# A fused attention and two-expert-layer kernel: V spread over partitions by way of DRAM, and the split of one half of the last rows at another step

## The chip, the cores and the metric

The kernel runs on one core of one Trainium2 chip. The metric is the device time of one execution in microseconds. The engines are named TensorE (PE; PEld is its weight load), VectorE (DVE), ScalarE (ACT), GpSimd (POOL) and SyncE (SP); SyncE issues most of the DMAs.

## The reference

Three stages follow one another. All sizes are fixed: batch 4, 8 heads, 576 positions, head dimension 64, 128 random features, model width 512, 8 experts.

```python
def phi(x):
    proj = np.einsum('bhsd,df->bhsf', x, w_phi)
    proj = proj - np.max(np.abs(proj), axis=-1, keepdims=True)
    return np.concatenate([np.exp(proj), np.exp(-proj)], axis=-1)
q_p, k_p = (phi(q), phi(k))
kv = np.einsum('bhsf,bhsd->bhfd', k_p, v)
z = np.sum(k_p, axis=2)
num = np.einsum('bhsf,bhfd->bhsd', q_p, kv)
den = np.einsum('bhsf,bhf->bhs', q_p, z)[..., None] + 1e-06
x = num / den                       # then heads side by side: [4, 576, 512]
...
h = x.transpose(0, 2, 1) @ U @ V    # U [576, 32], V [32, 576]: mixes positions
u = x + h.transpose(0, 2, 1)
x = u + np.maximum(u @ w_ch1, 0.0) @ w_ch2      # inner width 2048
...
# per position: an expert e of 8 (argmax, or the previous one's), its softmax share p
out[b, s] = p[e] * (np.maximum(x[b, s] @ w1[e], 0.0) @ w2[e])   # inner width 1024
```

U, V, `w_ch1` and `w_ch2` arrive in float64 and are narrowed on the chip.

## The kernel before

**Stages.** `attn_step(S_)` runs the attention as a software pipeline over 16 pairs of heads: projections (`proj`, tile `pj`), exponentials (`exp_k` into `ek`, `tq` into `eq`), `kv_mm`, `num`, then `t_mm` (tile `tps`, product with U) and `ut` (tile `utps`, transposed back to rows of features, plus the product with V). `ut` writes `y`, which holds u transposed: 512 features as 4 x 128 partitions, by 2304 rows (4 x 576 positions). Then `work()` runs the blocks of the two feed-forward layers: `mm1` multiplies by the first layer's weights into PSUM tile `psf`, `mm2` by the second's. Four units of weights are gone through by five blocks of 512, 512, 256, 512 and 512 rows each.

**Precision by halves.** A float32 value x is held as two reduced-precision numbers, `hi` (a cast of x) and `lo` (x minus `hi`), and each product takes three matmuls: weight-hi by hi, weight-hi by lo, weight-lo by hi (lines 537 to 539 and 556 to 558). So before `mm1` can read rows, those rows of `y` need a cast on ScalarE (`hi_a`, `hi_b`, line 510) and a subtraction on GpSimd (`lo_a`, `lo_b`, line 512, four instructions of 128 x 288). `split_rows(b, c)` does that for half c of batch b; half (3,0) are rows 1728 to 2015. `mm1` of the fourth block (rows 1280 to 1791) is the first that reads it. In the same way `mm1`'s results go to `hhi` (line 542, ScalarE) and `hlo` (line 543, VectorE), which `mm2` reads.

**V.** `load_uv` is a generator that `attn_step` and `prepare` advance: U and V are loaded, narrowed (VectorE, and an addition on GpSimd, line 76), and V, which arrives as 4 chunks of 144 columns, each on its own 32 partitions (`vq`), is spread so that each of four groups of 32 partitions holds all 576 columns (`v`). `vs` is its float32r form: the cast (line 273) in all groups, and in the second and fourth group the remainder (line 275). `ut` reads it from the seventh step on.

**The order of the work.** It is written out by hand. Each engine runs its instructions in the order of the program text. During `work()` the function `side(i, step)` places side work behind step 0 to 7 of block i: at steps 2 and 6 it takes the next entry of `splits`, and it advances the preparation of a weight tile (`w_prep`: conversions on VectorE, an addition into `cv_w` on GpSimd, a cast on ScalarE at line 173, a subtraction into `w` on GpSimd). At the end of the attention (1,1) and (2,0) are split at once, and `splits` holds (2,1), (3,0), (3,1). The first block is done by then, so the second block's steps take (2,1) and (3,0) and the third block's step takes (3,1).

**PSUM.** `tq`, `num`, `tps`, `utps` and V's products `vps` share one pool of three buffers (`ps_f`): each new tile waits until the tile three before it has been read. In the feed-forward stages five buffers go round.

Of the kernel before, what the change touches and what calls it, by code (L numbers as in the profile page):

```python
# [7 lines left out]
F32 = mybir.dt.float32  # L8
# [8 lines left out]
B, H, S, D, F = 4, 8, 576, 64, 128  # L17
# [22 lines left out]
def model(ctx, tc, kq, vx, wphi, ident, up, vp, wff, wg, wmoe, rconst, outT):  # L40
    nc = tc.nc
# [8 lines left out]
    dram = ctx.enter_context(tc.tile_pool(name="dram", bufs=1, space=bass.MemoryType.DRAM))  # L50
    ula_p = ctx.enter_context(tc.tile_pool(name="ula", bufs=1))
    ps_f = ctx.enter_context(tc.tile_pool(name="ps_f", bufs=3, space=PSUM))

    def f32(ap):
        return ap.bitcast(F32)

    id_sb = const.tile([128, 128], F32, name="id_sb")
# [163 lines left out]
    spare = y.rearrange("p k t -> p (k t)").rearrange("p (r s) -> p r s", s=S)  # L221
# [25 lines left out]
    def load_uv():  # L247


        u, v, vq = spare[:, 10, :160], spare[:, 14], spare[:, 11, :144]  # L250
        four = spare[:, 15, :512].rearrange("p (c r j) -> p c r j", c=4, r=4)
        u_load, u_convert = load_small(up, 128, 160)
        v_load, v_convert = load_small(vp, 128, 144)
        next(u_load)
        next(v_load)
        yield
        u_convert(u)
        for c in range(4):
            nc.gpsimd.tensor_copy(out=four[:, c], in_=id_sb[:, 32 * c:32 * c + 32].unsqueeze(1).to_broadcast([128, 4, 32]))
        u3 = u.rearrange("p (c r) -> p c r", c=5)  # L260
        for c in (0, 32):
            nc.gpsimd.tensor_copy(out=ur[:, :, c:c + 32], in_=u3)
        yield
        v_convert(vq)
        yield
        for h in range(2):
            ps = ps_f.tile([128, 2, 144], F32, tag="f", name="vps")
            for c in range(2):
                nc.tensor.matmul(ps[:, c], lhsT=four[:, 2 * h + c].rearrange("p r j -> p (r j)"), rhs=vq,
                                 start=(c == 0), stop=(c == 1), skip_group_check=True)  # L270
            nc.scalar.copy(out=v[:, 288 * h:288 * h + 288].rearrange("p (c s) -> p c s", c=2), in_=ps)
        yield
        nc.scalar.copy(out=vs, in_=v)
        for r in (slice(32, 64), slice(96, 128)):
            nc.gpsimd.tensor_tensor(out=vs[r], in0=v[r], in1=f32(vs[r]), op=ALU.subtract)

    early = [load_uv()]
    next(early[0])
    load_v(1)
# [422 lines left out]
    splits = []  # L702

    def side(i, step):

        u, _, _, c = blocks[i]
        if u.kind == "ffn":
            if splits and step in (2, 6):
                split_rows(*splits.pop(0))
            if u.g < 3:  # L710
                for _ in range(2 if step in (3, 7) else 1):
                    if not preps and room() and at["prep"] < min(8 * u.g + 16, 8 * u.g + 10 + 8 * c // 5 if u.g else 16):
                        preps.append(w_prep())
                    prep_step()
                if late:
                    w_ahead()
            else:
                if step == 0 and c > 1:
                    bg.append(route(c - 2))
                bg_step()  # L720
                if 0 not in pidx:
                    bg_step()
                if 0 in pidx and step in (1, 3, 4, 5, 7):
                    if at["prep"] < 8 * len(ffn_units) + 8 and room():
                        preps.append(w_prep())
                        drain(preps)
                        w_ahead()
        else:
            k = units.index(u)
            if i + 2 == n and step == 0:  # L730

                drain(bg)
                left = late["ul"].tile([1, 1], F32, name="left")
                late["left"] = late["ul"].tile([1, 1], I32, name="lefti")
                nc.vector.tensor_reduce(out=left, in_=late["flags"], axis=AX, op=ALU.add)
                nc.vector.tensor_copy(out=late["left"], in_=left)
            if u.b == 0 and u.g == 0 and c == 0 and step == 0:
                bg.append(route(3))
            bg_step()
            if c == 0 and step == 4 and u.g == 0:  # L740
                scale_row(u.b)
            if k + 1 < len(units) and at["prep"] < min(8 * (k + 2), 8 * k + 8 + 4 * c + (step + 1) // 2) and room():
                v = units[k + 1]
                if v.b not in pidx:
                    drain(bg)
                preps.append(w_prep())
                drain(preps)
                w_ahead()
# [81 lines left out]
    with tc.For_i(0, nl):  # L830
# [42 lines left out]
        ps = late["psr"].tile([128, 4], F32, tag="r1", bufs=2, name="l_mps")  # L873
# [3 lines left out]
        for c in range(2):  # L877
            sl = slice(c * CH, (c + 1) * CH)
            for k, into in ((0, yb[:, :, sl]), (1, ob[:, :, sl])):
                h, l = (f32(t)[:, :, bass.ds(at_[k][c] * CH, CH)] for t in ul[k])  # L880
# [6 lines left out]
        with tc.For_i(0, FT2) as j:  # L887
# [3 lines left out]
            for c in range(2):  # L891
                sl = slice(c * CH, (c + 1) * CH)
                ps = late["psg"].tile([128, CF], F32, tag="f", name="l_ps")[:, :CH]
# [4 lines left out]
                for d in range(4):  # L898
                    ps = ps_f.tile([128, CF], F32, tag="f", name="l_acc")[:, :CH]
# [79 lines left out]
```

## Time and profile before

| | |
|---|---|
| runs, us | 797.07, 797.0, 795.45; median 797.0 |
| profiled execution, us | 795.62, of which the span is 793.8 |
| busy share of the span | PE 98%, PEld 87%, DVE 57%, ACT 34%, POOL 24% |
| granted TensorE clock, mean | 0.996 |
| TensorE's share of the chain that ended last | 88% |

A time in the sections below counts from the start of the span. The chain that ended last is followed back from the last instruction, at each step to whatever released it. The busy shares are means over stages of different kinds: until about 205 us the attention runs, with VectorE and ScalarE close to full in its first part; behind it the feed-forward layers are nearly all TensorE.

### The profile page before, as it was taken

The page shows a single profiled execution, that of the slowest core. Times are in us where ns is not written, and L with a number is a line of the kernel's source. Part 1 is how long each engine was busy: PE and PEld are TensorE (multiplying, and loading weights), DVE is VectorE, ACT ScalarE, POOL GpSimd, SP SyncE. Part 2 cuts the span into 40 slices and gives each one's busy share as a digit, 9 for nine tenths or more (in the row PEclk, how much of TensorE's full clock was granted, in tenths as well). Part 3 has the DMA queues.
Part 4 walks back from the last instruction along what each step waited for, and adds up shares of the span by engine and source line. Part 5 has one row for each costly group of instructions (what it writes and reads, how often), then busy time and mean ns, then how long its engine had stood idle before and what let it go on. Part 6 is the DMA issues. An engine that isn't in the chain of part 4 may idle for free.

```text
span 793.8 us, 17863 instructions
## 1 busy us (share of the span) xinstructions
PE 780.9 (98%) x7492; PEld 694.3 (87%) x7492; DVE 454.9 (57%) x889; ACT 269.0 (34%) x589; POOL 190.9 (24%) x242
## 2 busy tenths in 40 slices
PE   8999999999999999999999999999999999999997
PEld 6899888988888888988889888887889999999997
DVE  7888999742675535544555443246567664434442
ACT  5667777741221111111111111122324433243340
POOL 1122424200474202230222302021204441202202
PEclk9999999999999999999999999999999999999999
DMA  6444434200012101110011100001222342343421
GB/s 198 149 123 142 130 112 143 64 2 2 27 53 78 44 12 53 54 54 23 30 54 54 54 0 1 1 1 39 58 69 70 103 127 90 110 131 110 128 71 62
DMA packets 25778, 56.04 MB, mean 71 GB/s; under 512 B 3616, under 2 KB 8864, under 8 KB 25696
## 3 DMA queue, kind: packets, MB, share of 16 engines
q1 hardware_dynamic: 21984, 51.28, 20.6%
q10 hardware_dynamic: 3456, 3.46, 1.3%
q8 instruction: 59, 0.97, 0.5%
q0 software_dynamic: 256, 0.15, 0.1%
q14 instruction: 23, 0.19, 0.1%
HBM read 50.01 MB, written 4.87 MB: 69 GB/s over the span
## 4 chain that ended last, share of the span: by engine, by line
PE 88%; DVE 7%; ACT 2%; POOL 2%; DMA 1%; issue 1%; DVEq 0%; ACTq 0%
PE psf L539 12%; PE psf L556 12%; PE psf L537 12%; PE psf L538 12%; PE psf L557 12%; PE psf L558 12%; PE kv L332 4%; PE num L366 3%; PE pj L299 3%; PE tq L346 2%; DVE pg L303 2%; DVE mx L302 1%; POOL lo_b L512 1%; PE utps L409 1%; PE tps L392 1%; PE utps L404 1%
## 5 line engine op out<-in xcount | busy, mean ns | idle before, releaser
L556 PE MATMUL psf<-hhi,w 128*128 128x512 f32 (+2 forms) x576 | 194.2, 337 | 0.0
L557 PE MATMUL psf<-hhi,w 128*128 128x512 f32 (+2 forms) x576 | 193.3, 336 | 0.3 <-DVE w L177 0.3
L558 PE MATMUL psf<-hlo,w 128*128 128x512 f32 (+2 forms) x576 | 193.1, 335 | 0.0
L543 DVE SCALAR_TENSOR_TENSOR hlo<-psf,hhi 128x512 fp32r<-128x512 f32 (+2 forms) x144 | 80.1, 556 | 178.4 <-ACT hhi L542 178.3
L542 ACT ACTIVATE hhi<-psf 128x512 fp32r<-128x512 f32 (+2 forms) x144 | 70.7, 492 | 261.8 <-PE psf L539 254.1
L556 PEld LDWEIGHTS psf<-hhi,w 128*128 128x128 f32 x576 | 108.3, 188 | 12.1 <-issue 1.4
L538 PE MATMUL psf<-lo_b,w 128*128 128x288 f32 (+2 forms) x352 | 116.0, 329 | 1.8 <-POOL lo_b L512 1.8
L557 PEld LDWEIGHTS psf<-hhi,w 128*128 128x128 f32 x576 | 108.3, 188 | 10.5 <-DVE w L177 0.5
L558 PEld LDWEIGHTS psf<-hlo,w 128*128 128x128 f32 x576 | 108.3, 188 | 10.3
L539 PE MATMUL psf<-hi_b,w 128*128 128x288 f32 (+2 forms) x352 | 116.4, 331 | 0.0
L537 PE MATMUL psf<-hi_b,w 128*128 128x288 f32 (+2 forms) x352 | 115.9, 329 | 0.1
L565 DVE TENSOR_TENSOR y<-psf,y 128x512 f32<-128x512 f32 (+2 forms) x112 | 65.4, 584 | 83.0 <-PE psf L558 82.6
L76 POOL TENSOR_TENSOR cv_w<-cv_w,cv_b 128x256 f32<-128x256 f32 x64 | 46.5, 748 | 207.0 <-DVE cv_b L92 207.0
L537 PE MATMUL psf<-hi_a,w 128*128 128x512 f32 (+1 forms) x224 | 79.1, 353 | 0.0
L539 PE MATMUL psf<-hi_a,w 128*128 128x512 f32 (+1 forms) x224 | 78.5, 350 | 0.0
L538 PE MATMUL psf<-lo_a,w 128*128 128x512 f32 (+1 forms) x224 | 78.1, 349 | 0.0
L538 PEld LDWEIGHTS psf<-lo_b,w 128*128 128x128 f32 x352 | 66.5, 189 | 8.0 <-POOL lo_b L512 2.1
L537 PEld LDWEIGHTS psf<-hi_b,w 128*128 128x128 f32 x352 | 66.5, 189 | 5.5 <-ACT hi_b L510 0.3
L539 PEld LDWEIGHTS psf<-hi_b,w 128*128 128x128 f32 x352 | 66.6, 189 | 5.3
L177 DVE TENSOR_TENSOR w<-raw,w 128x512 fp32r<-128x512 f32 x64 | 44.8, 700 | 37.4 <-ACT w L173 36.4
L568 POOL TENSOR_TENSOR y<-y,sbc 128x288 f32<-128x288 f32 x30 | 31.6, 1056 | 134.9 <-DVE y L565 134.9
L173 ACT CAST w<-cv_w 128x512 fp32r<-128x512 f32 x32 | 19.8, 618 | 122.9 <-POOL cv_w L76 122.8
(120 smaller groups left out, 1119.2 us busy)
## 6 DMA issues: line engine op xcount, KB each, us to landing
raw<-in_wff SPq DMA_DIRECT2D x32, 512.0 KB, 3.3
raw<-in_wmoe SPq DMA_DIRECT2D x64, 256.0 KB, 2.6
kq<-in_kq SPq DMA_DIRECT2D x14, 576.0 KB, 4.0
vt<-in_vx SPq DMA_DIRECT2D x16, 325.0 KB, 3.2
outT<-y ACTq DMA_DIRECT2D x23, 144.0 KB, 3.2
outT<-y SPq DMA_DIRECT2D x9, 144.0 KB, 1.8
sbc<-mine SPq DMA_DIRECT2D x4, 288.0 KB, 3.3
kq<-in_kq SPq DMA_DIRECT2D x3, 192.0 KB, 3.5
```

Of the source, the lines that this page charges most:

```text
L76: eng.tensor_tensor(out=dst[:, sl], in0=a[:, sl], in1=b[:, sl], op=op)
L177: nc.vector.tensor_tensor(out=w[:, 1], in0=f, in1=f32(w[:, 0]), op=ALU.subtract)
L332: nc.tensor.matmul(out[c], lhsT=e[:, half, i, c], rhs=rhs, start=(tl == 0 and half == 0), stop=(tl == 8 and half == 1), skip_group_check=True)
L537: nc.tensor.matmul(ps, lhsT=wh, rhs=hi[:, k], start=(k == 0), stop=False)
L538: nc.tensor.matmul(ps, lhsT=wh, rhs=lo[:, k], start=False, stop=False)
L539: nc.tensor.matmul(ps, lhsT=wl, rhs=hi[:, k], start=False, stop=(k == 3))
L542: nc.scalar.activation(out=hhi, in_=ps, func=ACTF.Relu)
L543: nc.vector.scalar_tensor_tensor(out=hlo, in0=ps, scalar=0.0, in1=f32(hhi), op0=ALU.max, op1=ALU.subtract)
L556: nc.tensor.matmul(ps, lhsT=wh, rhs=hhi, start=(f == 0), stop=False)
L557: nc.tensor.matmul(ps, lhsT=wl, rhs=hhi, start=False, stop=False)
L558: nc.tensor.matmul(ps, lhsT=wh, rhs=hlo, start=False, stop=(f == 3))
L565: nc.vector.tensor_tensor(out=dst, in0=ps, in1=dst, op=ALU.add)
```

## The change

V's chunks are written to a DRAM tile `vd` of 32 x 576 by four DMAs, and that tile is read into the four groups of partitions by four more; all eight are issued on GpSimd. The four products with copies of the identity (`four`), these copies, and the two copies out of PSUM go away. In `side`, the second of the two steps at which an entry of `splits` is taken is 4 instead of 6.

```diff
-        four = spare[:, 15, :512].rearrange("p (c r j) -> p c r j", c=4, r=4)
+        vd = dram.tile([32, S], F32, name="vd")
...
         u_convert(u)
-        for c in range(4):
-            nc.gpsimd.tensor_copy(out=four[:, c], in_=id_sb[:, 32 * c:32 * c + 32].unsqueeze(1).to_broadcast([128, 4, 32]))
...
         v_convert(vq)
-        yield
-        for h in range(2):
-            ps = ps_f.tile([128, 2, 144], F32, tag="f", name="vps")
-            for c in range(2):
-                nc.tensor.matmul(ps[:, c], lhsT=four[:, 2 * h + c].rearrange("p r j -> p (r j)"), rhs=vq,
-                                 start=(c == 0), stop=(c == 1), skip_group_check=True)
-            nc.scalar.copy(out=v[:, 288 * h:288 * h + 288].rearrange("p (c s) -> p c s", c=2), in_=ps)
+        for c in range(4):
+            nc.gpsimd.dma_start(out=vd[:, 144 * c:144 * c + 144], in_=vq[32 * c:32 * c + 32])
+        yield
+        for r in range(4):
+            nc.gpsimd.dma_start(out=v[32 * r:32 * r + 32], in_=vd)
         yield
         nc.scalar.copy(out=vs, in_=v)
...
-            if splits and step in (2, 6):
+            if splits and step in (2, 4):
```

The diff takes four lines away, so later lines have a number lower by four in the new kernel. The instructions move at two places, each shown on the two engines concerned.

ScalarE around V, before (`y<-vps` are the two copies out of PSUM, `vs<-y` is the cast of the spread V, names in brackets are the semaphores waited for, by engine):

```order
39 L310 ACTIVATE ek<-pg 128x384 [waits DVE_49]
40 L311 ACTIVATE ek<-pg 128x384
41 L271 COPY y<-vps 128x288 [waits PE_49] x2
42 L394 CAST ts<-tps 128x128 [waits PE_49]
43 L310 ACTIVATE ek<-pg 128x384 [waits DVE_49]
44 L311 ACTIVATE ek<-pg 128x384
45 L273 CAST vs<-y 128x576 [waits Activation_49]
46 L348 ACTIVATE eq<-tq 128x384 [waits PE_49]
```

and now:

```order
39 L306 ACTIVATE ek<-pg 128x384 [waits DVE_49]
40 L307 ACTIVATE ek<-pg 128x384
41 L390 CAST ts<-tps 128x128 [waits PE_49]
42 L306 ACTIVATE ek<-pg 128x384 [waits DVE_49]
43 L307 ACTIVATE ek<-pg 128x384
44 L269 CAST vs<-y 128x576 [waits DMASW6_49,DMASW7_49,DMASW5_49,DMASW4_49]
45 L344 ACTIVATE eq<-tq 128x384 [waits PE_49]
46 L345 ACTIVATE eq<-tq 128x384
```

The two copies are gone, and the cast of `vs` waits for four GpSimd-issued DMAs instead of a copy just ahead of it.

GpSimd around V, before (`y<-id_sb` are the copies of the identity, `y<-cv_a,cv_b` the additions that end the narrowing of U and of V):

```order
10 L76 TENSOR_TENSOR y<-cv_a,cv_b 128x80 x2
11 L259 COPY y<-id_sb 128x128 x4
12 L262 COPY ur<-y 128x5x32 x2
13 L76 TENSOR_TENSOR y<-cv_a,cv_b 128x72 x2
14 L275 TENSOR_TENSOR vs<-y,vs 32x576 x2
15 L76 TENSOR_TENSOR cv_w<-cv_w,cv_b 128x256 x2
16 L76 TENSOR_TENSOR w<-cv_w,w 128x256 x2
17 L76 TENSOR_TENSOR cv_w<-cv_w,cv_b 128x256 x2
18 L76 TENSOR_TENSOR w<-cv_w,w 128x256 x2
```

and now:

```order
10 L76 TENSOR_TENSOR y<-cv_a,cv_b 128x80 x2
11 L260 COPY ur<-y 128x5x32 x2
12 L76 TENSOR_TENSOR y<-cv_a,cv_b 128x72 x2
13 L264 DMA vd<-y 32x144 x4
14 L267 DMA y<-vd 32x576 x4
15 L271 TENSOR_TENSOR vs<-y,vs 32x576 x2
16 L76 TENSOR_TENSOR cv_w<-cv_w,cv_b 128x256 x2
17 L76 TENSOR_TENSOR w<-cv_w,w 128x256 x2
18 L76 TENSOR_TENSOR cv_w<-cv_w,cv_b 128x256 x2
```

The copies are gone; eight DMAs stand between V's narrowing and the remainder of `vs`, and the first read waits for all four writes.

ScalarE in the second block of the first feed-forward unit, before (`hi_b<-y` behind three `hhi` is half (3,0)):

```order
299 L510 CAST hi_b<-y 128x4x288 x3
300 L173 CAST w<-cv_w 128x512
301 L542 ACTIVATE hhi<-psf 128x256 x3
302 L510 CAST hi_b<-y 128x4x288
303 L173 CAST w<-cv_w 128x512
304 L542 ACTIVATE hhi<-psf 128x256
305 L542 ACTIVATE hhi<-psf 128x512
306 L173 CAST w<-cv_w 128x512
```

and now:

```order
298 L506 CAST hi_b<-y 128x4x288 x3
299 L173 CAST w<-cv_w 128x512
300 L538 ACTIVATE hhi<-psf 128x256
301 L506 CAST hi_b<-y 128x4x288
302 L538 ACTIVATE hhi<-psf 128x256 x2
303 L173 CAST w<-cv_w 128x512
304 L538 ACTIVATE hhi<-psf 128x256
305 L538 ACTIVATE hhi<-psf 128x512
306 L173 CAST w<-cv_w 128x512
```

The cast of half (3,0) has moved ahead of two `hhi`.

GpSimd at the same place, before (`lo_b<-y,hi_b` in the first row is half (2,1), in the fifth half (3,0)):

```order
41 L512 TENSOR_TENSOR lo_b<-y,hi_b 128x288 x4
42 L76 TENSOR_TENSOR cv_w<-cv_w,cv_b 128x256 x2
43 L76 TENSOR_TENSOR w<-cv_w,w 128x256 x2
44 L76 TENSOR_TENSOR cv_w<-cv_w,cv_b 128x256 x2
45 L512 TENSOR_TENSOR lo_b<-y,hi_b 128x288 x4
46 L76 TENSOR_TENSOR w<-cv_w,w 128x256 x2
47 L76 TENSOR_TENSOR cv_w<-cv_w,cv_b 128x256 x2
```

and now:

```order
42 L508 TENSOR_TENSOR lo_b<-y,hi_b 128x288 x4
43 L76 TENSOR_TENSOR cv_w<-cv_w,cv_b 128x256 x2
44 L76 TENSOR_TENSOR w<-cv_w,w 128x256 x2
45 L508 TENSOR_TENSOR lo_b<-y,hi_b 128x288 x4
46 L76 TENSOR_TENSOR cv_w<-cv_w,cv_b 128x256 x2
47 L76 TENSOR_TENSOR w<-cv_w,w 128x256 x2
48 L76 TENSOR_TENSOR cv_w<-cv_w,cv_b 128x256 x2
```

The four subtractions of half (3,0) have moved ahead of a `cv_w`, the addition that ends the conversion of the next weight tile. Half (3,1) stands where it stood.

## Rows read from the trace of the kernel before

**Rows 1.** Waits of TensorE, whole span: who for whom, total, times, longest.

```profile
PE psf L538 <- POOL lo_b L512: 1.8, 1, 1.8
```

**Rows 2.** Timeline, 219 to 230 us: start, duration, engine, line, operation [idle, releaser].

```profile
219.24 0.38 ACT L542 ACTIVATE hhi<-psf 128x256 fp32r<-128x256 f32 x1
...
219.41 1.45 POOL L76 TENSOR_TENSOR w<-cv_w,w 128x256 fp32r<-128x256 f32 x2 [0.73 <-ACT w L173]
...
221.57 1.15 ACT L510 CAST hi_b<-y 128x1152 fp32r<-128x1152 f32 x1
...
222.77 0.50 PE L537 MATMUL psf<-hi_b,w 128*128 128x512 f32 x1
...
222.88 1.41 POOL L76 TENSOR_TENSOR cv_w<-cv_w,cv_b 128x256 f32<-128x256 f32 x2 [2.02 <-DVE cv_b L92]
224.24 3.44 POOL L512 TENSOR_TENSOR lo_b<-y,hi_b 128x288 fp32r<-128x288 f32 x4
...
224.85 0.38 ACT L542 ACTIVATE hhi<-psf 128x256 fp32r<-128x256 f32 x1
...
229.22 0.28 PE L556 MATMUL psf<-hhi,w 128*128 128x256 f32 x1
```

**Rows 3.** Chain of waits, 224 to 248 us: start, duration, what.

```profile
225.89 0.43 PE psf L539
...
246.19 0.23 PE psf L556
```

**Rows 4.** Stretch 225 to 226 us: busy by engine, granted clock, DMA share, GB/s.

```profile
225.00:226.00 1.00, 0.90 (x2) 0.81 (x3) 0.74 (x2) 0.23 (x1) 1.00 (x3) 0.50 0.42 168
```

**Rows 5.** Timeline, 233 to 248 us, GpSimd, ScalarE and VectorE.

```profile
235.64 4.18 POOL L512 TENSOR_TENSOR lo_b<-y,hi_b 128x288 fp32r<-128x288 f32 x4
...
241.77 1.08 ACT L542 ACTIVATE hhi<-psf 128x512 fp32r<-128x512 f32 x2
...
245.79 0.68 DVE L543 SCALAR_TENSOR_TENSOR hlo<-psf,hhi 128x512 fp32r<-128x512 f32 x1
```

**Rows 6.** Timeline, 22 to 33 us, where V is spread.

```profile
23.27 0.63 POOL L76 TENSOR_TENSOR y<-cv_a,cv_b 128x72 f32<-128x72 f32 x2 [3.35 <-DVE den L376]
...
25.54 1.61 PE L269 MATMUL vps<-y 128*128 128x144 f32 x8
...
27.16 0.87 PE L392 MATMUL tps<-x,ur 128*64 128x128 f32 x10
...
28.40 1.15 PE L366 MATMUL num<-kvs,eq 128*64 128x65 f32 x32 [0.38 <-ACT y L271]
...
29.54 0.68 ACT L273 CAST vs<-y 128x576 fp32r<-128x576 f32 x1
...
30.36 2.86 POOL L275 TENSOR_TENSOR vs<-y,vs 32x576 fp32r<-32x576 f32 x2 [6.46 <-ACT vs L273]
...
32.24 0.49 ACT L348 ACTIVATE eq<-tq 128x384 f32<-128x384 f32 x1 [2.03 <-PE tq L346]
```

**Rows 7.** Timeline, 35 to 40 us.

```profile
35.81 0.63 ACT L382 ACTIVATE x<-num,den 64x64 f32<-64x64 f32 x2 [0.84 <-DVE x L378]
...
37.83 0.48 ACT L349 ACTIVATE eq<-tq 128x384 f32<-128x384 f32 x1
...
38.43 0.49 PE L346 MATMUL tq<-id_sb,pg 128*128 128x128 f32 x3
```

**Rows 8.** GpSimd's transfers into `mine`: duration of the issue, ns, minimum, median, maximum.

```profile
L662 POOL DMA_DIRECT2D mine<-r_tp x4: 543/554/704, 545.4 to 643.4; - x4
```

**Rows 9.** The same into `sall`, and their time from issue to landing.

```profile
L663 POOL DMA_DIRECT2D sall<-r_tp x4: 521/521/527, 546.1 to 644.0; - x4
...
DMA to landing us min/median/max: 1.8/2.6/3.4
```

**Rows 10.** Two stretches, columns as in rows 4.

```profile
25.00:26.00 1.00, 0.91 (x20) 0.80 (x16) 0.90 (x2) 0.96 (x4) 0.00 (x0) 1.00 1.03 417
28.00:29.00 1.00, 0.62 (x21) 0.60 (x22) 0.69 (x2) 1.00 (x5) 0.00 (x0) 1.00 0.00 0
```

## The prediction

> **What bounds the kernel now.** I read the page's busy shares first: TensorE is busy nearly throughout (the table ahead), so a change can win only what TensorE waits for, its instructions, or its clock. Next the waits of TensorE over the whole span: behind the start's load, one wait stands out, 1.8 us of a first-layer product for `lo_b`, written by GpSimd [rows 1]. The rest are 0.4 us or less. Then the timeline at both edited places, and the chain of waits there. Around 225 us the chain runs through GpSimd: it prepares a weight (`cv_w`), then splits rows 1728 to 2015, here called half (3,0), and only then can the product go on [rows 2]. The wait also costs clock: in 225 to 226 us the granted clock is 0.50, that is the 1.2 GHz level, though a microsecond-scale wait is all that went before [rows 4], and a product that takes 0.23 us elsewhere takes 0.43 us [rows 3]. Around 25 us TensorE, ScalarE and VectorE are all close to full, and from the `num` at 28.40 us the chain goes over TensorE almost without a break.
>
> **Edit 2, half (3,0) two steps sooner.** Of the three halves left in `splits` only (3,0) moves: the others are taken in step 2 either way. Its cast to `hi_b` on ScalarE then comes behind the first `hhi` of that block instead of the third, and its four `lo_b` subtractions on GpSimd ahead of the next `cv_w`.
>
> What goes: the product that uses the half takes from 222.77 us to 229.22 us, 6.45 us [rows 2]. Twelve matmuls at 0.23 us [rows 3] are 2.76 us. So 3.7 us can be won at most, 1.8 us of it wait [rows 1], the rest clock.
>
> What it takes: the cast starts when the first `hhi` ends, 219.24 + 0.38 = 219.62 us, and lasts 1.15 us, to 220.8 us. GpSimd ends its `w` at 219.41 + 1.45 = 220.86 us. The four subtractions then run from 220.9 us for 3.44 us [rows 2], to 224.3 us; with VectorE busy beside them four took 4.18 us [rows 5], to 225.1 us. The product begins at 222.77 us and wants its first quarter at once, ready at about 221.8 us, and the fourth after ten matmuls, 225.1 us. No wait there, though only just with the longer time. The two `hhi` that the cast passes are 1.15 us later at most; their products come over 3 us on.
>
> What is late next: `cv_w` is now behind the subtractions, 224.3 + 1.41 = 225.7 us. ScalarE has the cast of that weight ahead of the block's last `hhi`; before, `hhi` began 224.85 - 224.29 = 0.56 us after `cv_w`. So it comes at 226.3 us (227.1 us with the longer subtractions) and is there 0.4 us later. TensorE, done with its product at 225.5 us, does nine matmuls of 256 columns in half of 0.23 us each and asks for it at 226.6 us, for its remainder `hlo` at 226.9 us. A new wait of 0.2 to 0.9 us, say 0.4, leaves 3.3 us.
>
> A second cap comes 20 us on. The second-layer product that begins at 246.19 us [rows 3] needs its last `hlo` after 11 matmuls, at 248.7 us; VectorE writes that from 245.79 us to 246.47 us [rows 5]. This `hlo` hangs on a sequence over GpSimd (half (3,1), 235.64 us, then a weight), ScalarE (`hhi`, 241.77 us) and VectorE, not on TensorE, so only its slack of 248.7 - 246.5 = 2.25 us is safe. VectorE gets the last `hhi` of the earlier block 1.8 us later than before, but does its conversions with less GpSimd work beside them. I put the sequence 0.4 us sooner; bounds are 0.5 us later and 1.0 us sooner. So edit 2 gives 2.25 + 0.4 = **2.7 us**, between 1.7 and 3.3 us.
>
> **Edit 1, V by way of DRAM.** Removed: four copies on GpSimd at 18 us, under no wait; the four `vps` products (eight records); two evictions on ScalarE. TensorE goes from `vps` at 25.54 us to `num` at 28.40 us, 2.86 us, of which `tps` is 0.87 us [rows 6]. Without the rest TensorE would be 2.0 us ahead. That is the upper end of this edit.
>
> Added: eight DMAs on GpSimd's queue, four writes, a wait for all four, four reads; and ScalarE's cast of `vs` now waits for the four reads. Behind it in ScalarE's order stand the `eq` and `ek` that TensorE's next steps need. No such transfer stands in this stretch of the trace; the nearest rows are GpSimd's transfers of 8 rows late in the kernel: 0.52 us to issue, 0.70 us for the first [rows 8, 9], 1.8 to 3.4 us from issue to landing, median 2.6 us [rows 9]. With 32 rows I take 0.6 us to issue. GpSimd has V in float32 at 23.27 + 0.63 = 23.9 us [rows 6]. The last of four writes starts three issues later, 25.7 us, and lands 2.2 us on, at 27.9 us; the last read starts 1.8 us later, 29.8 us, and lands at 32.1 us, with 2.4 us for its larger size. Written with an issue of c us and two landings, the sum is 23.9 + 6c + two landings.
>
> The cast takes 0.68 us [rows 6], so it ends at 32.8 us instead of 30.2 us. From the first `eq` behind it (32.24 us) to the end of the last `eq` (37.83 + 0.48 us) [rows 6, 7] ScalarE needs 6.1 us, of which 0.84 us is a wait for VectorE [rows 7] that would vanish: 5.2 us. TensorE's `tq` at 38.43 us [rows 7] needs that buffer, and there every lead is given back: the `eq` ends at landing + 0.68 + 5.2, so against 38.3 us the edit wins 32.4 minus the landing. With 32.1 us this is **+0.3 us, taken as 0.2**. Both landings at 1.8 us and 0.52 us per issue give 30.6 us, +1.8 us; both at 3.4 us and 0.6 us give 34.3 us, -1.9 us. GpSimd's subtractions behind the cast (2.86 us [rows 6]) end near 35.8 us, before that last `eq`, so they set nothing; what else stands behind GpSimd's new wait is a weight not due before 45 us, so that wait costs nothing by itself.
>
> The DMA engines are at a share of 1.03 in 25 to 26 us [rows 10], when the writes start. The Trainium skill, page "DMA: Bandwidth & Descriptors", section "Issuing engines are not separate DMA queues", says that transfers from all queues run on the same 16 engines and interleave, which speaks against this edit and for the long landings; by it the writes would take 3.4 us and the edit would lose 0.9 us. The same page's SWDGE anatomy gives about 2.0 us plus bytes over 436e3; an estimate from it is 2.04 us for a write and 2.17 us for a read, and then the edit wins 0.7 us.
>
> **Sum.** 2.7 + 0.2 = 2.9 us. The profiled execution took 795.6 us (span 793.8 us), so 792.7 us against it. The three runs have a median of 797.0 us and reach down to 795.45 us; the mean of these four is 796.3 us, and I set the forecast at 796.3 - 2.9 = 793.4 us. About 0.2%, 1.6 us, is what a measurement here can tell from no change.
>
> **Rivals.**
> A. Forecast: 793.4 us, chance 0.52.
> B. Both gains in full: the trip lands by 30.4 us and ScalarE is not waited for, 2.0 us, and the sequence before 246 us moves along, 3.3 us: 791.0 us. For it: the DMA engines have a share of 0.00 in 28 to 29 us [rows 10], and half of the trip lies about there. Against: it wants the shortest rows for all. Chance 0.12.
> C. The gains are mostly replaced by new waits: edit 2 leaves 1.7 us because `hhi` and `hlo` of the weight sequence do not move, edit 1 loses 1 us in a loaded queue: 795.6 us, within 0.2%. For it: the caps are real and near. Chance 0.25. That half (3,0) is not ahead of the weight after all would belong here too, but the order of instructions shows it there.
> D. Slower: the price of a transfer's issue on GpSimd grows with its rows, 32 against 8. At four times 0.53 us, 2.1 us each, the sum is 23.9 + 12.6 + 4.6 = 41.1 us; ScalarE stands still until then, the edit loses 8.7 us, and edit 2 brings back 2.7 us: 802.3 us. It decides from c = 1.4 us: there the landing is 36.9 us, the loss 4.5 us, and the total is past 0.2%. For it: the trace has no 32-row issue on this queue. Against: the two sizes seen issue alike, and the first issue's extra is 0.2 us. A long standstill could also drop the clock as at 225 us, for 1 to 2 us more. Chance 0.11.
>
> **How the numbers follow.** Faster by over 0.2%: most of A, all of B, a quarter of C: 0.66. Within: the rest of C and a little of A: 0.24. Slower: 0.10. The range leaves out D and half of B: 791.6 to 796.8 us.
>
> **What would show it.** In the new profile: the wait for `lo_b` of (3,0) gone from TensorE's list and the clock at 1.00 through that stretch; a shorter wait, under 1 us, for `hhi` or `hlo` a few microseconds later, and perhaps one before the product that was at 246 us. Near 32 us ScalarE's cast of `vs` waiting for DMA, by 2 to 3 us; issues of 0.5 to 0.7 us on GpSimd; the `tq` that stood at 38.43 us within 1 us of that. Wrong if the issues are much longer, if the cast ends after 34 us, or if the clock drops in either place.

## The result

The changed kernel takes 802.4 us (median of 4 runs, 801.4 to 803.1), the kernel before 796.4 us in runs beside it: a ratio of 1.0072 with a 95% interval of 1.0057 to 1.0087. It is slower by 6.0 us, where 793.4 us was forecast and 796.8 us was the upper end of the range. The profiled execution took 802.58 us with a span of 800.8 us, 7.0 us more than the span before.

The waits of TensorE over the span of the changed kernel (who for whom, total, times, longest):

```profile
PE kv L328 <- ACT kvs L332: 5.3, 1, 5.3
...
PE psf L552 <- ACT hhi L538: 0.5, 1, 0.5
...
PE psf L554 <- DVE hlo L539: 0.2, 1, 0.2
```

The wait of 1.8 us for `lo_b` [rows 1] is gone, and 0.5 us for `hhi` and 0.2 us for `hlo` have come in its place, as the prediction said. But there is a new first row, three times as long as the one that went: the products `kv` wait once, for 5.35 us, for `kvs`, a name that the prediction never mentions.

The stretch around V in the changed kernel (start, duration, engine, line, operation, in brackets the idle time ahead and what ended it), to be read against rows 6 and 7:

```profile
25.36 2.18 POOL L264 DMA_DIRECT2D vd<-y  x4 [0.31 <-POOL y L76]
...
31.41 1.96 POOL L267 DMA_DIRECT2D y<-vd  x4 [3.87 <-DMA vd<-y]
...
34.02 0.40 PE L369 MATMUL num<-kvs,eq 128*64 128x65 f32 x8
...
37.25 0.67 ACT L269 CAST vs<-y 128x576 fp32r<-128x576 f32 x1 [6.60 <-DMA y<-vd]
...
39.32 0.40 ACT L332 COPY kvs<-kv 128x260 f32<-128x260 f32 x1
...
39.77 1.57 PE L328 MATMUL kv<-vt,ek 128*64 128x65 f32 x24 [5.35 <-ACT kvs L332]
41.27 2.36 PE L295 MATMUL pj<-wphi_sb,kq 64*64 64x128 f32 x48
```

Read it from the end. TensorE finishes `num` at 34.42 us and stands until 39.77 us, because `kv`, the accumulator of the next pair, has a single buffer in PSUM and is free only when ScalarE has copied the last pair's sums out of it (`kvs`). That copy itself depends on nothing late. But ScalarE takes its instructions in the order of the program, and five places ahead of it stands the cast of `vs`, which waits 6.60 us for DMA. In the kernel before, the cast ran at 29.54 us [rows 6] with nothing to wait for.

The transfers of the same stretch (duration of an issue in ns: minimum, median, maximum; then the time from issue to landing of all eight):

```profile
L264 POOL DMA_DIRECT2D vd<-y x4: 503/518/687, 25.4 to 27.0; - x4
L267 POOL DMA_DIRECT2D y<-vd x4: 496/496/498, 31.4 to 32.9; - x4
...
DMA to landing us min/median/max: 3.8/4.5/5.0
```

The issues cost about what rows 8 and 9 had shown, 0.50 to 0.69 us, although there are 32 rows to a transfer instead of 8. The landings do not: the shortest of the eight, 3.8 us, is longer than the longest of rows 9, 3.4 us.

The chain of waits of the same stretch has the two legs as its longest pieces (start, duration, what):

```profile
27.04 3.81 DMA vd<-y
...
32.87 4.28 DMA y<-vd
```

And the stretches behind TensorE's stop (columns as in rows 4: busy time by engine, then granted clock, DMA share, GB/s):

```profile
39.00:40.00 1.00, 0.23 (x4) 0.23 (x6) 0.00 (x0) 1.00 (x4) 0.93 (x2) 0.80 0.00 0
...
41.00:42.00 1.00, 1.00 (x24) 0.88 (x24) 0.00 (x0) 0.98 (x3) 0.00 (x0) 0.50 0.06 16
42.00:43.00 1.00, 1.00 (x24) 1.00 (x20) 0.10 (x1) 0.01 (x1) 0.00 (x0) 0.50 0.00 0
```

TensorE comes back at the lower of its two levels (0.50, 1.2 GHz) and stays there for about three microseconds: 48 rows of `pj` take 2.36 us, against 1.54 us in the kernel before.

Edit 2 can be read at its own place, to compare with rows 2:

```profile
226.81 1.15 ACT L506 CAST hi_b<-y 128x1152 fp32r<-128x1152 f32 x1
...
228.11 4.19 POOL L508 TENSOR_TENSOR lo_b<-y,hi_b 128x288 fp32r<-128x288 f32 x4
...
229.78 0.39 PE L533 MATMUL psf<-hi_b,w 128*128 128x512 f32 x1
...
232.27 1.42 POOL L76 TENSOR_TENSOR cv_w<-cv_w,cv_b 128x256 f32<-128x256 f32 x2
...
232.93 0.28 PE L552 MATMUL psf<-hhi,w 128*128 128x256 f32 x1
...
234.25 0.87 ACT L538 ACTIVATE hhi<-psf 128x256 fp32r<-128x256 f32 x2
234.68 0.39 PE L552 MATMUL psf<-hhi,w 128*128 128x256 f32 x1 [0.53 <-ACT hhi L538]
```

The product that took 6.45 us from 222.77 us [rows 2] now runs from 229.78 to 232.93 us, 3.15 us. `cv_w` stands behind the subtractions, and `hhi` behind it comes late by 0.53 us.

To see where the 7 us arise, take the same instruction of VectorE in both profiles and subtract its start before from its start now (worked out from the two traces):

| at (us of before) | now - before | what lies between |
|---|---|---|
| 14 | +1.15 | the start's load |
| 36.5 | -0.38 | the `vps` products are gone: 1.5 us won |
| 56 | +7.39 | stop 5.35, low clock 1.5, a gap of TensorE of 0.7 with no cause shown |
| 231 | +7.36 | nothing |
| 300 | +5.51 | edit 2: 1.85 us won |
| 612 | +5.51 | nothing |
| 789 | +6.41 | waits for expert weights, see below |

The start is not the change's: in the twelve profiles of this study this first number lies anywhere between 0 and 3.3 us, and the changed part of the program has not begun there. So edit 1 lost 6.2 us by 56 us, edit 2 won 1.85 us, and 0.9 us more is lost late. The last 0.6 us of the 7.0 lie behind the last row, where GpSimd's closing instruction takes 1.37 us instead of 0.71; nothing of the change stands there.

### The profile page after: what moved, and what is told of

Same layout as the page of the kernel before. It is cut to its first block, busy times and chain, and to the rows that moved or that the text cites. A ratio compares the mean times of both kernels' runs of the same rounds, so it can differ in the third digit from the quotient of the medians.

```text
span 800.8 us, 17865 instructions
## 1 busy us (share of the span) xinstructions
PE 782.4 (98%) x7484; PEld 694.4 (87%) x7484; DVE 454.0 (57%) x889; ACT 268.1 (33%) x587; POOL 194.1 (24%) x246
## 4 chain that ended last, share of the span: by engine, by line
PE 81%; DVE 9%; POOL 4%; ACT 2%; DMA 2%; issue 1%; ACTq 0%; DVEq 0%; POOLq 0%
PE psf L552 11%; PE psf L554 11%; PE psf L553 11%; PE psf L535 11%; PE psf L533 11%; PE psf L534 11%; PE kv L328 3%; PE pj L295 3%; PE num L362 3%; POOL lo_b L508 2%; PE tq L342 2%; DVE pg L299 1%; DVE mx L298 1%; PE utps L405 1%; PE tps L388 1%
```

## Experiments

The theory that the experiments test: edit 2 wins some 2 us as predicted; edit 1 loses some 8 us, because two landings of 4 to 5 us in a row hold the cast, the cast holds `kvs` on ScalarE, TensorE stops for `kvs`, and its clock falls. Rivals: the transfers cost by loading the DMA engines; they cost because GpSimd issues them; the low clock costs nothing; the cast only happens to stand beside the stop. Times below are medians, and ratios are against the kernel before in runs on the same chip.

**The two edits apart.** First the kernel before with the step alone:

```diff
-            if splits and step in (2, 6):
+            if splits and step in (2, 4):
```

> The second edit alone: V is spread by products as before, the split of half (3,0) comes at step 4. Theory T (the loss is the wait of ScalarE for V's trip, and the rows' edit wins): the trace after shows 3.7 us won at the product that reads the half and about half of that given back at hhi and hlo behind it, so 796.4 - 1.9 = 794.5 us, between 793.5 and 795.3. Rival R2 (the rows' edit costs part of the loss, by the new waits it makes): 796.4 us or more.

Measured 794.6 us, ratio 0.9982 (0.9972 to 0.9991): 1.9 us faster. From the waits of TensorE in its profile:

```profile
PE psf L556 <- ACT hhi L542: 0.5, 1, 0.5
...
PE psf L558 <- DVE hlo L543: 0.2, 1, 0.2
```

And from its timeline, the `hlo` that the prediction named as a second cap:

```profile
246.42 0.68 DVE L543 SCALAR_TENSOR_TENSOR hlo<-psf,hhi 128x512 fp32r<-128x512 f32 x1
```

In the kernel before this `hlo` began at 245.79 us [rows 5]. This profile runs 0.6 us later from its start on, so the `hlo` has not moved at all, while everything on TensorE ahead of it has; TensorE waits 0.2 us for it, and what was won beyond its slack is given back there. Now edit 1 alone, with the step left at 6:

```diff
-            if splits and step in (2, 4):
+            if splits and step in (2, 6):
```

> The first edit alone: V by way of DRAM, half (3,0) split at step 6 as before. T: the loss of both edits plus what the rows win, 802.4 + 1.9 = 804.3 us. R2: 796 to 799 us.

Measured 804.5 us, ratio 1.0089 (1.0070 to 1.0108): 8.0 us slower. Its waits:

```profile
PE kv L328 <- ACT kvs L332: 5.6, 1, 5.6
PE psf L534 <- POOL lo_b L508: 1.8, 1, 1.8
```

The stop for `kvs` is there without edit 2, and the old wait for `lo_b` is back. The two differences, +8.0 and -1.9 us, add up to 6.1 us, against 6.0 us for both: as far as four runs of edit 1 alone can tell, the edits don't disturb each other.

**The transfers without anyone waiting.** The kernel before, products and all, plus the same eight transfers at the same places; the reads go to a second DRAM tile that nobody uses:

```diff
+        vd = dram.tile([32, S], F32, name="vd")
+        sink = dram.tile([128, S], F32, name="sink")
+        for c in range(4):
+            nc.gpsimd.dma_start(out=vd[:, 144 * c:144 * c + 144], in_=vq[32 * c:32 * c + 32])
         yield
+        for r in range(4):
+            nc.gpsimd.dma_start(out=sink[32 * r:32 * r + 32], in_=vd)
```

> The kernel before with the eight transfers added at the same places on GpSimd, but read into a DRAM tile that nothing reads; V is still spread by products, so no engine but GpSimd waits for them. T: nothing is lost by the transfers as such, 796.4 us within 0.2%; their landings are again 4 to 5 us. Rival R1 (the transfers disturb the shared DMA engines, the early loads or GpSimd's own work): 799 to 802 us.

Measured 796.6 us, ratio 1.0001 (0.9991 to 1.0010). The transfers as such, their issues on GpSimd and their load on the DMA engines cost at most 0.8 us, the upper end of this interval. Their landings were shorter here (the reads end in DRAM instead of SBUF, so the size of a landing is not to be carried over from this run):

```profile
DMA to landing us min/median/max: 2.5/3.2/4.0
```

This profile has a second use. It has the wait for `lo_b` of the kernel before, and yet the clock did not fall behind it (a stretch, columns as in rows 4):

```profile
227.00:228.00 1.00, 1.00 (x5) 0.68 (x5) 0.89 (x3) 0.00 (x0) 1.00 (x2) 1.00 0.07 25
```

TensorE stood 1.85 us until 226.71 us and went on at 1.00; after the same wait of 1.83 us the clock was 0.50 in the profile of before [rows 4]. Whether the clock falls behind this wait, then, differs between profiles, although the program is the same there.

**One landing instead of two.** The changed kernel, with the reads taken from an input that is ready, so that rows of `kq` stand where V should and no read waits for the writes:

```diff
-            nc.gpsimd.dma_start(out=v[32 * r:32 * r + 32], in_=vd)
+            nc.gpsimd.dma_start(out=v[32 * r:32 * r + 32], in_=kq[0, 32 * r:32 * r + 32, 0:S])
```

> The changed kernel with its four reads taken from rows of the input kq instead of from vd, so that they need not wait for the four writes (the values of V are then other numbers, the work is the same). Theory (the two landings in a row put the vs cast at 37.25 us and the cast holds kvs): the reads are issued at 27.5 to 29.5 us instead of 31.4 to 33.4 us, land 3.9 us sooner, the cast runs at 33.4 to 34.0 us, kvs at 35.5 to 35.9 us, TensorE's wait for kvs is 1.5 to 1.9 us instead of 5.35, and 796.8 to 799 us. Rival (the price is something other than the wait for the second landing, such as the transfers' load on the DMA engines): 801.5 to 802.5 us.

Measured 794.9 us, ratio 0.9984 (0.9971 to 0.9996): 7.5 us better than the changed kernel, and better than either theory said. The reads, the cast and the products `kv`:

```profile
29.68 1.96 POOL L267 DMA_DIRECT2D y<-in_kq  x4
...
33.87 0.67 ACT L269 CAST vs<-y 128x576 fp32r<-128x576 f32 x1 [1.04 <-DMA y<-in_kq]
...
36.39 0.92 PE L328 MATMUL kv<-vt,ek 128*64 128x65 f32 x24 [0.34 <-ACT kvs L332]
```

The reads follow the writes without a pause, the cast comes 4.2 us after the first of them, and the stop shrinks from 5.35 to 0.34 us. I had expected 1.5 us or more; this profile starts 2.2 us later than that of the changed kernel, and the landings are shorter (3.0 to 4.2 us for the writes). Counted from the first write's issue, the cast comes 5.5 us sooner than in the changed kernel: 3.9 us because the reads need not wait for the writes, and 1.7 us because the last read lands 2.62 us after its issue instead of 4.28 us. Same number of transfers, same issuer, same instructions on the other engines: most of the price is that the second landing follows on the first.

**Another issuer.** The changed kernel with all eight transfers on SyncE:

```diff
-            nc.gpsimd.dma_start(out=vd[:, 144 * c:144 * c + 144], in_=vq[32 * c:32 * c + 32])
+            nc.sync.dma_start(out=vd[:, 144 * c:144 * c + 144], in_=vq[32 * c:32 * c + 32])
...
-            nc.gpsimd.dma_start(out=v[32 * r:32 * r + 32], in_=vd)
+            nc.sync.dma_start(out=v[32 * r:32 * r + 32], in_=vd)
```

> The changed kernel with the eight transfers of V issued by SyncE instead of GpSimd, in the same step; the loads of vt, kq and raw stand between and behind them there. Theory A (GpSimd's own queue makes the landings of 3.8 to 5.0 us): landings near 2.2 us on SyncE, V in place by 32.5 us, no wait for kvs, 794.5 to 796.5 us. Theory B (the trip through DRAM is that slow beside the loads of kq, vt and raw, whoever issues it): landings of 3.8 to 4.5 us, the cast at about 36.5 us, the wait for kvs 4 to 5 us, 800 to 802 us.

Measured 798.9 us, ratio 1.0032 (1.0019 to 1.0045), between the two theories, with single runs from 795.0 to 800.7 us. The profiled execution is the fastest of them, so its rows bound the matter from below only. The writes are issued from 24.2 us, the reads from 27.3 us. The landings, of the four writes and of the four reads:

```profile
DMA to landing us min/median/max: 1.5/1.6/1.6
...
DMA to landing us min/median/max: 3.5/3.9/4.7
```

And the stretches in which the first writes and the last reads are under way (columns as in rows 4):

```profile
25.00:26.00 1.00, 0.91 (x28) 0.80 (x26) 0.90 (x2) 0.91 (x3) 0.00 (x0) 1.00 0.14 37
...
29.00:30.00 1.00, 1.00 (x37) 0.83 (x30) 0.93 (x4) 0.76 (x2) 0.00 (x0) 1.00 0.97 383
```

The writes land in 1.5 to 1.6 us, where GpSimd's took 3.8 us and more. But the issuer is not all that differs: in SyncE's order the loads of `vt` and `kq` now stand behind the writes, so that these run at a DMA share of 0.14, while in the changed kernel the loads had left before and the share was 0.80 to 1.03 from 25 to 28 us. The reads, behind those loads, run at 0.97 and take 3.5 to 4.7 us, as on GpSimd. So on SyncE the landings go with the load of their stretch, as theory B has it, though the reads are also four times as large and stand behind those loads in SyncE's own order. What SyncE gained, 3.5 us by the medians, came with a new order of the loads, and even in this fastest execution TensorE stops for `kvs`, for 2.9 us. GpSimd as issuer does not make a long landing by itself either: in the direct copies below its transfers of 18 KB, which end in SBUF and run at a DMA share of 0.20 to 0.27, land with a median of 2.1 us.

But the load is not the whole price of the changed kernel's trip. Two stretches of that kernel ahead of the landing of the last write, which comes at 30.85 us (columns as in rows 4):

```profile
29.00:30.00 1.00, 1.00 (x38) 0.93 (x37) 0.96 (x4) 0.65 (x3) 0.00 (x0) 1.00 0.04 5
30.00:31.00 1.00, 0.89 (x29) 0.64 (x23) 0.97 (x3) 0.65 (x2) 0.00 (x0) 1.00 0.00 0
```

And all queues that moved a packet from 31.4 to 34.3 us, behind the issue of the first read at 31.41 us (packets, MB, share of 16 engines):

```profile
q1 hardware_dynamic: 110, 0.51, 57.0%
q8 instruction: 1, 0.02, 2.0%
```

In the last 1.85 us of the writes' leg the DMA engines are next to idle. And GpSimd's transfers, which run in the queue `software_dynamic`, are not in the second list: of the four reads, none has a packet under way for 2.9 us from the first issue, although the DMA share from 31 to 32 us is 0.06. What they wait for there, no run shows, so that GpSimd's queue has a price of its own beside these loads is not excluded.

**The cast behind `kvs`.** The changed kernel, with the cast of `vs` and its subtractions one step later in the order:

```diff
+        yield
         yield
         nc.scalar.copy(out=vs, in_=v)
...
-        if S_ in (3, 4):
+        if S_ in (3, 4, 5):
```

> The changed kernel with the vs cast and its subtraction a step later on ScalarE and GpSimd, behind the copy kvs of pair 2 instead of ahead of it; the transfers stay where they are. Theory (the cast that waits for the second landing holds the copy kvs, for which alone TensorE stands): no wait for kvs; the next reader of V is utps, whose product with vs then waits for GpSimd's subtraction, which ends at 40.9 us (38.01 + 2.87 us in the changed kernel) where TensorE comes at about 37 us: a wait of some 4 us there, utps at 40.9 instead of 44.1 us, 797.7 us with the clock kept and 799.2 us with it halved for some 3 us. Rival (TensorE's stop comes from something else that the cast only accompanies): a wait for kvs stays, 802.4 us.

Measured 800.7 us, ratio 1.0060 (1.0036 to 1.0084): 1.5 us above the upper end of the theory and 1.7 us below the rival, so the time alone does not decide. The rows show the theory's course to the half microsecond (its profiled execution took 799.4 us, of which 1.5 us are lost late in the kernel, see below):

```profile
32.39 0.41 ACT L333 COPY kvs<-kv 128x260 f32<-128x260 f32 x1
...
36.39 0.67 ACT L270 CAST vs<-y 128x576 fp32r<-128x576 f32 x1 [2.76 <-DMA y<-vd]
...
37.15 3.20 POOL L272 TENSOR_TENSOR vs<-y,vs 32x576 fp32r<-32x576 f32 x2 [4.45 <-ACT vs L270]
...
40.40 0.51 PE L406 MATMUL utps<-vs,ts 128*128 128x256 f32 x2 [4.12 <-POOL vs L272]
```

`kvs` runs at 32.39 us, TensorE has no wait there, and the transfers, which land in 3.6 to 4.3 us, are felt where V is really used: 4.12 us at `utps`, and again the low clock behind it. The place of the cast in the order decided whom the late landing stops. It also says that moving the cast by a step could not have saved the edit.

**The clock by itself.** The changed kernel with products of `wphi` by itself into a spare `pj` buffer, which nobody reads, ahead of the products that stand (NFILL is 36):

```diff
+        if G == 9:
+            fill = ps_a.tile([128, 2, 4, 128], F32, tag="pj", bufs=2, name="pj")
+            for _ in range(NFILL):
+                for c in (0, 64):
+                    for n_, r in enumerate((slice(0, 64), slice(64, 128))):
+                        nc.tensor.matmul(fill[c:c + 64, n_, 0], lhsT=wphi_sb[r, 0:64], rhs=wphi_sb[r], start=True, stop=True)
```

> The changed kernel with 144 extra small products on TensorE (copies of wphi against itself into a spare pj buffer that nobody reads) right ahead of the kv products of pair 3, where it stands for 5.35 us. They take the place of the stop at 34.3 to 39.2 us and change nothing else. 48 such products take 1.54 us, so 144 take some 4.6 us at full clock. Theory (the stop itself costs 5.35 us and the granted clock of 0.50 between 39.6 and 43.0 us another 1.5 to 2.2 us): kvs still comes at 39.3 us, the clock stays at 1.00 through 40 to 43 us, 800.2 to 800.9 us. Rival (the low clock lies beside other waiting and costs nothing): 802.4 us.

Measured 803.5 us, ratio 1.0084 (1.0063 to 1.0104), a miss by my own arithmetic: I had counted rows of the profile as products, and each of these products has two rows. The filler ran on long past `kvs` (two rows of TensorE's timeline; idle time for which the profile shows no releaser is put down to "issue"):

```profile
34.79 4.80 PE L323 MATMUL pj<-wphi_sb 64*64 64x128 f32 x165
41.74 3.71 PE L323 MATMUL pj<-wphi_sb 64*64 64x128 f32 x123 [2.15 <-issue]
```

So once more at half the size (NFILL = 18 instead of 36).

> The filler of e4 at half its size: 72 products, which stand as 144 rows in a profile (each of these products has two rows: in e4 144 of them ran as 288 rows, for 8.5 us). 48 such rows take 1.54 us, so these take 4.6 us, about the 5.35 us of TensorE's stop, and end before kvs. Theory (the stop costs what its wait says and the clock of 0.50 behind it 1.5 to 2.2 us more): clock 1.00 between 39 and 46 us, 800.2 to 800.9 us. Rival (the low clock costs nothing): 802.4 us.

Measured 800.2 us, ratio 1.0045 (1.0031 to 1.0059): 2.2 us better than the changed kernel, though TensorE has more to do. From the timeline of TensorE:

```profile
35.08 4.16 PE L323 MATMUL pj<-wphi_sb 64*64 64x128 f32 x144
40.89 0.92 PE L335 MATMUL kv<-vt,ek 128*64 128x65 f32 x24 [1.65 <-ACT kvs L339]
```

And the stretch behind the stop (busy time by engine, granted clock, DMA share, GB/s):

```profile
41.00:42.00 1.00, 1.00 (x32) 0.93 (x36) 0.00 (x0) 0.99 (x4) 1.00 (x1) 1.00 0.00 0
```

TensorE is busy for most of what was its stop, the clock stays at 1.00, and the 24 rows of `kv` take 0.92 us instead of 1.57 us. So the clock that falls behind the stop costs about 1.5 us by the rows of `kv` and `pj`, and up to 2.2 us by the medians, in which other differences lie too (late in the kernel this profile loses 0.1 us, that of the changed kernel 0.9). The rest of the some 8 us that edit 1 costs is the stop of 5.35 us, less the 1.5 us won by the dropped products, the gap of 0.7 us and the loss late in the kernel; for the last two no cause is shown.

**Can the edit be saved?** Two attempts. First, V is narrowed ahead of U and so a step sooner, written in one transfer and read in four:

```diff
-        vd = dram.tile([32, S], F32, name="vd")
+        vd = dram.tile([128, 144], F32, name="vd")
...
+        next(v_load)
         next(u_load)
-        next(v_load)
         yield
+        v_convert(vq)
+        nc.gpsimd.dma_start(out=vd, in_=vq)
         u_convert(u)
...
```

> Both edits, but V is narrowed ahead of U, one step sooner, near 18 us instead of 24 us, and written to DRAM by one transfer instead of four, the reads stay four. T: V is there by 18.2 us, the write lands 4.5 us on near 23 us, the last read is issued 1.6 us later and lands near 29 us, about when ScalarE comes to its cast; no wait of more than 1 us, no loss of clock, and the 2.0 us of the dropped products stay won: 796.4 - 1.9 - 1.5 = 793 us, between 792 and 794.5. R1: over 798 us, since the same bytes move. If V by DRAM is worth nothing even when it is not waited for: 794.5 us, as the rows' edit alone.

Measured 796.7 us, ratio 1.0001 (0.9992 to 1.0011), no better than before; I had expected 793 us. ScalarE's cast in its timeline:

```profile
31.62 0.67 ACT L269 CAST vs<-y 128x576 fp32r<-128x576 f32 x1 [0.53 <-DMA y<-vd]
```

And TensorE's idle times around it:

```profile
24.82 0.89 PE L295 MATMUL pj<-wphi_sb,kq 64*64 64x128 f32 x24 [0.85 <-DVE pg L299]
31.91 0.87 PE L295 MATMUL pj<-wphi_sb,kq 64*64 64x128 f32 x20 [1.07 <-issue]
```

The cast waits only 0.53 us, and there is no stop for `kvs`. The trip itself is no quicker: the longest of its five landings takes 6.7 us. It only starts sooner. But TensorE now waits 0.85 us for VectorE's `pg`, ahead of which the narrowing of V and of U stand one behind the other; TensorE has a gap of 1.07 us for which the profile shows no releaser, and 1.5 us more go late in the kernel (below). Second, V goes from SBUF to SBUF in sixteen transfers, with one landing and no DRAM:

```diff
+        for c in range(4):
+            for r in range(4):
+                eng = (nc.gpsimd, nc.sync)[r % 2]
+                eng.dma_start(out=v[32 * r:32 * r + 32, 144 * c:144 * c + 144], in_=vq[32 * c:32 * c + 32])
...
```

> The changed kernel with V's quarters copied from SBUF to SBUF, sixteen transfers (each row group r gets each column group c straight from vq), without DRAM and without the second landing: the eight of even r pairs issued on GpSimd, eight on SyncE. Output as before. Theory (one landing instead of two takes the price away, as in e5): issued from 25.1 to some 29 us (8 at 0.5 us on GpSimd), landed by 33 to 34 us, the cast then, a wait for kvs of 0 to 1 us, 794.0 to 796.0 us; that is no better than the four products with the identity (the kernel with the moved step alone, 794.6 us). Rival (sixteen transfers of rows of 576 bytes clog the queues): landings of 5 us and more, a wait for kvs of over 2 us, 797 to 801 us.

Measured 797.2 us, ratio 1.0009 (0.9998 to 1.0021), 1.2 us over the upper end of my theory and just inside the rival's range. From its timeline, the landings of the sixteen, and the KB and median landing of GpSimd's eight:

```profile
33.35 0.67 ACT L268 CAST vs<-y 128x576 fp32r<-128x576 f32 x1 [2.76 <-DMA y<-y]
...
35.87 0.92 PE L327 MATMUL kv<-vt,ek 128*64 128x65 f32 x24 [2.05 <-ACT kvs L331]
...
DMA to landing us min/median/max: 1.7/2.3/3.2
...
y<-y POOLq DMA_DIRECT2D x8, 18.0 KB, 2.1
```

The landings are short, against the rival's reason, and the cast comes at 33.35 us, as the theory said; the chain of waits up to it goes over SyncE, which needs 5.73 us, from 25.00 us on, to issue its eight. But TensorE stops for 2.05 us all the same, the rival's figure by another road, and in the stretch behind it the clock is at 0.50 for over two microseconds. TensorE was there at 33.82 us, while `kvs` has the cast and four `eq` ahead of it on ScalarE and ended at 35.82 us. No form of the edit that I tried beats the kernel with the moved step alone, 794.6 us, which is faster than both kernels of this case.

**Left open: the end of the kernel.** Every kernel of this study without the `vps` products lost a little more on the kernel before after 612 us, 0.1 to 2.2 us by its profile (0.9 us in the changed kernel); the two that still have them lost nothing. TensorE waits there for expert weights (`w`), whose loads' longest landing between 585 and 628 us was 3.2 to 3.8 us in most of the former and 2.9 to 3.0 us in the latter. But the two kernels with the filler, which lack the `vps` products as well, had 2.9 and 3.0 us too. No part of that stretch of the program is edited. I have no cause for it.

## Why the prediction was wrong

- **Edit 2** was right in mechanism and in its waits: half (3,0) in time, `cv_w` pushed back, a new wait for `hhi` (0.4 us predicted, 0.53 measured), and the cap at the product that stood at 246 us. The gain was put at 2.7 us, between 1.7 and 3.3, and is 1.9 us. The mis-sized term is the cap: I let the sequence behind `hlo` come 0.4 us sooner, it did not move, and the slack was about 1.9 us, not 2.25. Part of the 3.7 us to be won was also less sure than the rows looked, since the clock does not fall behind the old wait in every profile.
- **Edit 1, the issues**: c was taken as 0.6 us, measured 0.50 to 0.69 us. Rival D, the one on the slower side, hung on this term alone, and fell. The kernel came out at 802.4 us, nearly D's 802.3 us, by another road: that is luck. (The last read's start, 29.8 us in the text, is 29.7 us by its own terms; nothing follows from it.)
- **Edit 1, the landings: this is the step that failed.** Counted from the end of the wait chain, the last write took 3.8 us and the last read 4.3 us, 8.1 us together instead of 2.2 + 2.4 = 4.6. Even my outer bound, twice 3.4 us, was too short. These 3.5 us, and two pauses of GpSimd that the sum had left out (0.31 us ahead of the first write's issue, 0.56 us between the last write's landing and the first read's issue), less 0.5 us for cheaper issues, turn the sum's +0.3 us into -3.6 us. The rows were of transfers of 8 rows late in the kernel [rows 9]; the writes here start in a stretch with a DMA share of 1.03 before [rows 10] and of 0.80 now, and I gave that row no weight in the sum, though it was the row of this place. The page "DMA: Bandwidth & Descriptors" of the Trainium skill says in "Issuing engines are not separate DMA queues" that transfers of all queues run on the same 16 engines and interleave; the long landings among the loads agree with it in direction, and the loss that I put beside that sentence, 0.9 us, was a small part of the real one. With SyncE as issuer the writes, ahead of the loads, landed in 1.5 to 1.6 us and the reads, among them, in 3.5 to 4.7 us, which agrees with it again; the 1.85 us in which the last write is still out with the DMA engines next to idle are not explained by it. The estimate from the same page's SWDGE anatomy, 2.04 and 2.17 us, was about half of what was measured, 3.8 and 4.3 us, and the measurement decides. How much of the long landings is load, and what the rest is, stays open.
- **Edit 1, who waits.** I let TensorE meet ScalarE's delay at `tq`, at 38.43 us [rows 7], where a lead could be given back. It meets it four microseconds sooner, at `kv`, since `kvs` stands behind the same cast and the accumulator has one buffer. With the measured landing, the prediction's own formula gives a loss of 3.6 us (the cast's data at 37.15 us, less the later start of 1.15, against 32.4); the rows show 6.2 us. The wrong meeting place is little of that difference: the stop of 5.35 us less the 1.5 us won is 3.8 us. The rest is the clock, 1.5 us, and the gap of 0.7 us. The prediction's own sign of being wrong, a cast that ends after 34 us, came true: it ends at 37.92 us.
- **The clock** stood in the prediction as a remark under rival D, "1 to 2 us more". It belongs into every case with a long stop, at least as a chance, since one stop of 2.94 us was not followed by it; here it cost 1.5 us by the rows, up to 2.2 us by the filler.
- **The chances**: slower had 0.10, since its whole case rested on issues. A second slow case, two long landings under load, had its row in the trace and no chance of its own; C gave it 1 us.

## What to carry to other kernels

Where an in-order engine gets an instruction that waits for a DMA, go down its list and find the first thing behind it that another engine needs, above all a copy that frees a single-buffered accumulator; in this kernel the delay was paid there, not at the reader of the data. Price a transfer from rows of the stretch in which it runs, not from a quiet one, and a trip through DRAM as two landings and two waits in a row. Work on an engine that is already full may be cheaper than a wait: the products and two evictions, 2 us in all, had cost less than the trip that replaced them.

## What the runs showed of the hardware

- Landings of the trip's transfers, 18 and 72 KB each, took 3.8 to 5.0 us from GpSimd beside the loads of the start in the changed kernel, and 3.6 to 5.6 us in the four others with the same transfers; from SyncE 1.5 to 1.6 us at a DMA share of 0.14 and 3.5 to 4.7 us at 0.97; transfers of 18 KB from SBUF to SBUF took 1.7 to 3.2 us at 0.20 to 0.27; 8-row transfers late in the kernel took 1.8 to 3.4 us.
- In the changed kernel no packet of GpSimd's reads moved in the first 2.9 us from the first read's issue.
- The issue of a transfer on GpSimd cost 0.50 to 0.69 us for 32 rows and 0.52 to 0.70 us for 8 [rows 8, 9].
- The wait of TensorE for `lo_b`, 1.83 to 1.85 us, was followed by a granted clock of 0.50 in two profiles (the kernel before, edit 1 alone) and of 1.00 in a third (the transfers that nobody waits for); stops of 2.05 us (the direct copies), 4.12 and 5.35 us were followed by 0.50, one of 2.94 us (the profile with SyncE) and a gap of 2.15 us (the longer filler) were not.
- Gaps of TensorE of 0.7 to 2.2 us for which the profile shows no releaser came in several kernels, one of them in the middle of products that depend on nothing.
